# Gate and value products by Strassen's scheme in single PSUM banks, with twelve attention visits a batch

## Chip, cores, metric

One core of one Trainium2 chip. The metric is device microseconds of one execution. A ratio is the mean time of one kernel's fast runs over that of the other's fast runs of the same rounds, so it is not quite the ratio of the medians quoted.

## The reference

Sigmoid attention (8 batches, 12 heads, 448 tokens, head size 64), followed by a gated feed-forward over the 3584 tokens:

```python
scores = scale * q @ k.T - log(S);  attn = 1 / (1 + exp(-scores));  x = attn @ v
gate = maximum(x @ w_gate, 0);  val = x @ w_val        # x: 3584 x 768, w: 768 x 1536
out  = (gate * val) @ w_out                            # w_out: 1536 x 768
```

## The kernel before

The feed-forward of batch b and the attention of batch b + 1 are interleaved on TensorE: the loop over the feed-forward's matmuls calls `visit()` now and then. A "pass" is four 64x64 matmuls of scores and one sigmoid of 128x896. Three blocks of four heads make a batch; a block has seven score passes and seven value passes.

```python
def up(b, f, ...):                      # one chunk of 128 of d_ff: 6 gate + 6 value matmuls of 448
    for dc in range(NDC): gate = gv_part(b, f, wg, [dc]) ...
    nc.vector.tensor_scalar(out=g_sb, in0=gate, scalar1=0.0, op0=AOP.max)
    for dc in range(NDC): val = gv_part(b, f, wv, [dc]) ...
    nc.vector.tensor_tensor(out=hT[f][:, o:o+S], in0=g_sb, in1=val, op=AOP.mult)

def feed(i):                            # behind score pass i: what the next blocks need
    n, c = divmod(i, NCH); m = n + 1
    if c == 0 and NPRO <= m < NB: cast_block(m)                  # GpSimd
    ...
    if c == 3 and NPRO <= m < NB: dma_transposes(m)              # k, q of the next block, SP's queue
    if c == 3 and NPRO <= m + 1 < NB: load_all(m + 1)            # k, q, v of the one after, SP's queue

def visit():                            # three score passes, with the seven value passes when due
    ...
# per batch 7 visits (8 in batch 0), spread evenly over up() and down()
```

`down(col0)` makes 128 output rows (12 matmuls of 512, 12 of 256), VectorE evicts them and SP's queue stores them. Batches have alternately three and four such blocks: 0, 2, 4, 6 have three.

## Time and profile before

| | before |
|---|---|
| time | 429.98 us (429.91 to 430.1) |
| TensorE busy, share of the chain that ended last | 98%, 93% |
| VectorE, ScalarE, GpSimd busy | 39%, 42%, 24% |
| transposing transfers of k and q, issue to landing (median) | 3.0 us |

The chain that ended last is followed back from the last instruction, at each step to what released it. An issue is the instruction by which a queue starts a transfer; the transfer has landed when its data is there. In the lines below SPq is SP's queue, x18 a count, and L146 line 146 of the kernel.

```profile
105.30 1.23 SPq L146 DMA_TRANSPOSE kT<-h16k  x1
106.57 1.30 SPq L146 DMA_TRANSPOSE qT<-h16q  x1
107.92 0.58 SPq L90 DMA_DIRECT2D st_k<-in_k_dram  x1
108.54 0.48 SPq L90 DMA_DIRECT2D st_q<-in_q_dram  x1
109.07 0.47 SPq L90 DMA_DIRECT2D st_v<-in_v_dram  x1
```

```profile
kT<-h16k SPq DMA_TRANSPOSE x18, 3.0
qT<-h16q SPq DMA_TRANSPOSE x18, 3.0
```

The two transposes of the next block are issued first, then the three loads of the block after next, 1.4 MB.

### The profile page before, as it was taken

The page shows a single profiled execution, that of the slowest core. Times are in us where ns is not written, and L with a number is a line of the kernel's source. Part 1 is how long each engine was busy: PE and PEld are TensorE (multiplying, and loading weights), DVE is VectorE, ACT ScalarE, POOL GpSimd, SP SyncE. Part 2 cuts the span into 40 slices and gives each one's busy share as a digit, 9 for nine tenths or more (in the row PEclk, how much of TensorE's full clock was granted, in tenths as well). Part 3 has the DMA queues.
Part 4 walks back from the last instruction along what each step waited for, and adds up shares of the span by engine and source line. Part 5 has one row for each costly group of instructions (what it writes and reads, how often), then busy time and mean ns, then how long its engine had stood idle before and what let it go on. Part 6 is the DMA issues. An engine that isn't in the chain of part 4 may idle for free.

```text
span 428.4 us, 7873 instructions
## 1 busy us (share of the span) xinstructions
PE 418.1 (98%) x3282; PEld 216.5 (51%) x3282; DVE 166.5 (39%) x276; ACT 178.5 (42%) x217; POOL 102.2 (24%) x137
## 2 busy tenths in 40 slices
PE   7789999999999999999999999999999999999996
PEld 4334555544555445545455444554455544555553
DVE  3555542353323452244423444244422435235531
ACT  5952566525434445444343545443435363500000
POOL 2567683333300333013120233003330030000000
PEclk9999999999999999999999999999999999999999
DMA  8999996673535753386623666247443730030014
GB/s 303 384 385 385 390 373 155 184 196 115 160 98 103 205 149 113 78 206 174 170 50 94 179 173 173 73 95 207 121 150 98 181 72 0 20 93 0 2 37 110
DMA packets 64371, 66.96 MB, mean 156 GB/s; under 512 B 35792, under 2 KB 54608, under 8 KB 64336
## 3 DMA queue, kind: packets, MB, share of 16 engines
q1 hardware_dynamic: 63088, 64.63, 51.8%
q10 hardware_dynamic: 1248, 1.84, 1.2%
q8 instruction: 25, 0.41, 0.4%
q14 instruction: 10, 0.08, 0.1%
HBM read 47.19 MB, written 11.01 MB: 136 GB/s over the span
## 4 chain that ended last, share of the span: by engine, by line
PE 93%; ACT 3%; DMA 2%; DVE 1%; issue 0%; ACTq 0%; DVEq 0%
PE gv_ps L232 51%; PE y_ps L275 26%; PE qk_ps L173 8%; PE pv_ps L197 7%; ACT PT L183 3%; DMA st_q<-in_q_dram 2%; PE tr L159 1%; DVE ysb L289 0%; DVE gate_sb L249 0%; DVE xT L213 0%; DVE h16q L107 0%; ACT L367 0%; ACT xT L211 0%; ACTq L295 0%; ACTq L90 0%
## 5 line engine op out<-in xcount | busy, mean ns | idle before, releaser
L183 ACT ACTIVATE PT<-qk_ps,bias_t 128x896 f16<-128x896 f32 x168 | 159.2, 1008 | 191.1 <-PE qk_ps L173 191.1
L232 PE MATMUL gv_ps<-xT,wg 128*128 128x448 f16 x576 | 128.1, 353 | 0.4 <-ACT xT L211 0.2
L232 PE MATMUL gv_ps<-xT,wv 128*128 128x448 f16 x576 | 126.9, 353 | 0.0
L275 PE MATMUL y_ps<-wo,hT 128*128 128x512 f16 (+2 forms) x684 | 113.7, 323 | 0.0
L275 PEld LDWEIGHTS <-hT 128*128 128x128 f16 x684 | 64.6, 98 | 48.0 <-issue 6.3
L249 DVE TENSOR_SCALAR gate_sb<-gv_ps 128x448 f32<-128x448 f32 x96 | 59.9, 624 | 73.4 <-PE gv_ps L232 73.4
L256 DVE TENSOR_TENSOR hT<-gate_sb,gv_ps 128x448 f16<-128x448 f32 x96 | 59.6, 621 | 64.3 <-PE gv_ps L232 64.2
L232 PEld LDWEIGHTS <-wg 128*128 128x128 f16 x576 | 55.0, 98 | 55.7 <-issue 7.7
L232 PEld LDWEIGHTS <-wv 128*128 128x128 f16 x576 | 55.0, 98 | 54.8 <-issue 5.2
L289 DVE TENSOR_SCALAR ysb<-y_ps 128x512 f32<-128x512 f32 (+2 forms) x56 | 31.1, 555 | 105.3 <-PE y_ps L275 104.1
L107 POOL CAST h16q<-st_q 128x896 f16<-128x896 f32 x20 | 18.6, 930 | 220.0 <-DMA st_q<-in_q_dram 195.3
L173 PE MATMUL qk_ps<-qT,kT 64*64 64x448 f16 x672 | 48.6, 358 | 3.9 <-ACT PT L183 2.9
L197 PE MATMUL pv_ps<-PT,v 64*64 64x448 f16 x672 | 39.1, 350 | 0.8 <-ACT PT L183 0.7
L173 PEld LDWEIGHTS <-kT 64*64 64x64 f16 x672 | 16.5, 105 | 29.8 <-issue 22.7
L197 PEld LDWEIGHTS <-v 64*64 64x64 f16 x672 | 19.9, 107 | 12.7 <-issue 2.1
L211 ACT ACTIVATE xT<-pv_ps 128x448 f16<-128x448 f32 x43 | 21.0, 547 | 6.0 <-PE pv_ps L197 4.8
L287 ACT ACTIVATE ysb<-y_ps 128x128 f32<-128x128 f32 x1 | 0.3, 277 | 44.8 <-PE y_ps L275 44.8
L107 POOL CAST h16k<-st_k 128x896 f16<-128x896 f32 x20 | 18.6, 928 | 0.0
L114 POOL CAST v<-st_v 128x448 f16<-128x448 f32 x24 | 13.3, 556 | 10.3 <-DMA st_v<-in_v_dram 10.3
L115 POOL CAST v<-st_v 64x448 f16<-64x448 f32 x24 | 13.4, 558 | 1.5
L116 POOL CAST v<-st_v 64x448 f16<-64x448 f32 x24 | 13.3, 555 | 1.0
L139 POOL CAST wv<-st_wu 128x1536 f16<-128x1536 f32 x6 | 8.8, 1467 | 5.7 <-DMA st_wu<-in_moe_w_val_dram 5.7
(26 smaller groups left out, 59.3 us busy)
## 6 DMA issues: line engine op xcount, KB each, us to landing
out_dram<-ysb SPq DMA_DIRECT2D x54, 192.0 KB, 2.7
st_q<-in_q_dram SPq DMA_DIRECT2D x23, 448.0 KB, 4.5
st_v<-in_v_dram SPq DMA_DIRECT2D x23, 448.0 KB, 5.2
st_k<-in_k_dram SPq DMA_DIRECT2D x22, 448.0 KB, 4.0
st_wg<-in_moe_w_gate_dram SPq DMA_DIRECT2D x6, 768.0 KB, 12.3
st_wu<-in_moe_w_val_dram SPq DMA_DIRECT2D x6, 768.0 KB, 12.2
st_wo<-in_moe_w_out_dram SPq DMA_DIRECT2D x6, 768.0 KB, 12.1
st_v<-in_v_dram ACTq DMA_DIRECT2D x1, 448.0 KB, 5.8
```

What stands on the lines that cost most here:

```text
L107: eng.tensor_copy(o, i)
L114: eng.tensor_copy(t[:, 0], st[:, 0])
L115: eng.tensor_copy(t[0:64, 1], st[64:128, 1])
L173: nc.tensor.matmul(ps[o : o + 64, bank, 0:S], kT[r : r + 64, c, h, :], qT[r : r + 64, :, h, :], start=True, stop=True, tile_position=(r, o ...
L183: nc.scalar.activation(pt[:], ps[:, :, 0:S], AF.Sigmoid, bias=bias_t[:], scale=qk_scale)
L197: nc.tensor.matmul(pv[o : o + 64, pr, 0:S], t[r : r + 64, pr, c * D : (c + 1) * D], pt[r : r + 64, pr, :], start=(c == 0), stop=(c == NCH ...
L211: nc.scalar.activation(x[:], pv[:, pr, 0:S], AF.Copy, scale=XSCALE)
L232: nc.tensor.matmul(begun[key][:, 0:S], w[j][:, dc, jj * P : (jj + 1) * P], xT[b, dc][:], start=(dc == 0), stop=(dc == NDC - 1),)
L249: nc.vector.tensor_scalar(out=g_sb[:], in0=gate[:, 0:S], scalar1=0.0, scalar2=None, op0=AOP.max)
L256: nc.vector.tensor_tensor(out=hT[f][:, o : o + S], in0=g_sb[:], in1=val[:, 0:S], op=AOP.mult)
L275: nc.tensor.matmul(y[:, 0:w], hT[f][:, o : o + P], wo[f // FG][:, f % FG, c0 : c0 + w], start=(f == 0), stop=(f == NFC - 1),)
L289: nc.vector.tensor_scalar(out=dst, in0=y[:, 0:w], scalar1=OUT_SCALE, scalar2=None, op0=AOP.mult)
```

## The change

Intent: for batches 1 to 7, split the tokens (224 + 224), the contraction (384 + 384) and the outputs (gate, value) in halves and form the four results from seven half-size products instead of eight. The sums of weights are made once, in batch 0's output products; the sums of tokens once a batch; the seven products are combined by VectorE (five adds and one max-and-multiply per pair of chunks), ScalarE (a copy and a relu) and GpSimd (one multiply). The products need four single PSUM banks, so scores have two pairs of banks instead of three, so a visit has two score passes instead of three, and a batch twelve visits instead of seven.

```diff
-    qkp = ...(name="qkp", bufs=3, PSUM)   # pairs of banks: scores, values
-    wkp = ...(name="wkp", bufs=2, PSUM)   # single banks: gate, value, output
+    pairs = [psp.tile([P, 2, 512], FP32, name=f"pair{i}") for i in range(2)]
+    banks = [psp.tile([P, 512], FP32, name=f"bank{i}") for i in range(4)]
+        factors = {1: (A11, B(wg, 0)), 2: (A12, B(wg, 1)), 3: (S4, B(wv, 1)), 4: (A22, TT(4)),
+                   5: (S1, TT(1)), 6: (S2, TT(2)), 7: (S3, TT(3))}
+        todo = [(0, 1), (0, 6), (0, 7), (0, 2), (0, 5), (1, 1), (0, 3)]        # (pair of chunks, product)
+        for g in range(1, NG2):
+            todo += [(g, 6), (g - 1, 4), (g, 7), (g, 5), (g, 2)]
+            todo += [(g + 1, 1)] if g + 1 < NG2 else []
+            todo += [(g, 3)]
+        todo += [(NG2 - 1, 4)]
...
     def feed(i: int):
-        if c == 0 and NPRO <= m < NB:
-            cast_block(m)
-        if c == 3 and NPRO <= m < NB:
-            dma_transposes(m)
+        if NPRO <= m < NB:
+            if c == 0: cast_qk(m, "q", nc.gpsimd)
+            if c == 2: cast_qk(m, "k", nc.gpsimd)
+            if c == 4:
+                dma_transposes(m)
+                cast_v(m, nc.gpsimd)
         if c == 3 and NPRO <= m + 1 < NB:
             load_all(m + 1)
...
+            for _, may in gv_fast(b):                 # may: behind product 6 of each pair, six a batch
+                if may and b + 1 < B: visit()
+            todo = [0.3 + k * (total - 3.3) / 5 for k in range(6)]    # six more in the output products
```

More of the change, by code (lines that the diff above doesn't have):

```diff
@@ L49 @@
     wpool = ctx.enter_context(tc.tile_pool(name="wpool", bufs=1))
-    stp = ctx.enter_context(tc.tile_pool(name="stp", bufs=10))
+    stp = ctx.enter_context(tc.tile_pool(name="stp", bufs=9))
     swp = ctx.enter_context(tc.tile_pool(name="swp", bufs=5))
@@ L54, with next_pair, take, give @@
     qkTp = ctx.enter_context(tc.tile_pool(name="qkTp", bufs=4))
-    PTp = ctx.enter_context(tc.tile_pool(name="PTp", bufs=11))
-    xTp = ctx.enter_context(tc.tile_pool(name="xTp", bufs=2 * NDC))
-    gsbp = ctx.enter_context(tc.tile_pool(name="gsbp", bufs=3))
-    ysbp = ctx.enter_context(tc.tile_pool(name="ysbp", bufs=3))
-    qkp = ctx.enter_context(tc.tile_pool(name="qkp", bufs=3, space=bass.MemoryType.PSUM))
-    wkp = ctx.enter_context(tc.tile_pool(name="wkp", bufs=2, space=bass.MemoryType.PSUM))
+    PTp = ctx.enter_context(tc.tile_pool(name="PTp", bufs=8))
+    xTp = ctx.enter_context(tc.tile_pool(name="xTp", bufs=4))
+    sxp = ctx.enter_context(tc.tile_pool(name="sxp", bufs=1))
+    tmpp = ctx.enter_context(tc.tile_pool(name="tmpp", bufs=2))
+    ysbp = ctx.enter_context(tc.tile_pool(name="ysbp", bufs=2))
+    psp = ctx.enter_context(tc.tile_pool(name="psp", bufs=1, space=bass.MemoryType.PSUM))
+    pairs = [psp.tile([P, 2, 512], FP32, name=f"pair{i}") for i in range(2)]
+    banks = [psp.tile([P, 512], FP32, name=f"bank{i}") for i in range(4)]
+    held: set = set()
+    turn = {"pair": 0, "bank": 0, "banks": (0, 1)}
+    def next_pair():
+        turn["pair"] ^= 1
+        return pairs[turn["pair"]]
+    def take():
+        ids = turn["banks"]
+        for k in range(len(ids)):
+            i = ids[(turn["bank"] + k) % len(ids)]
+            if i not in held:
+                turn["bank"] = (turn["bank"] + k + 1) % len(ids)
+                held.add(i)
+                return i
+        raise AssertionError("no bank")
+    def give(i):
+        held.remove(i)
     bias_t = const.tile([P, 1], FP32, name="bias_t")
@@ L73 @@
     wo = [wpool.tile([P, FG, DM], FP16, name=f"wo{j}") for j in range(NG)]
-    hT = [wpool.tile([P, NHALF * S], FP16, name=f"hT{f}") for f in range(NFC)]
+    hT = [wpool.tile([P, 2, NHALF * S], FP16, name=f"hT{f}") for f in range(NFC // 2)]
     staged: dict = {}
@@ L87, in load_block @@
         for nm, src, c0, c1, eng in which:
-            st = stp.tile([P, 2, S], FP32, tag="st", name=f"st_{nm}")
+            if nm == "k2":
+                st = staged["k", n]
+            else:
+                st = stp.tile([P, 2, S], FP32, tag="st", name=f"st_{nm}")
             rows = src[b, i * HB : (i + 1) * HB].rearrange("(r h) (p c) d -> (h p) r (c d)", h=2, c=NCH)
@@ L153, in transposes @@
         if n <= NBLK:
-            tr = wkp.tile([P, NCH, 2, KC], FP16, tag="wk", name="tr")
-        else:
-            tr = qkp.tile([P, 2, 512], FP32, tag="qk", name="tr")[:, 0, 0 : S].bitcast(FP16)
-            tr = tr.rearrange("p (c h k) -> p c h k", c=NCH, h=2)
+            bank = take()
+            tr = banks[bank][:, 0:S]
+        else:
+            bank = None
+            tr = next_pair()[:, 0, 0:S]
+        tr = tr.bitcast(FP16).rearrange("p (c h k) -> p c h k", c=NCH, h=2)
         for c in range(cut[0], cut[-1]):
@@ L165, in transposes @@
                 eng.tensor_copy(t2[:, c0:c1], tr[:, c0:c1])
+        if bank is not None:
+            give(bank)
         qkT[nm, n] = t2
@@ L169, in scores @@
         qT, kT = qkT["q", n], qkT["k", n]
-        ps = qkp.tile([P, 2, 512], FP32, tag="qk", name="qk_ps")
+        ps = next_pair()
         for r, h, o, bank in ((0, 0, 0, 0), (0, 1, 64, 0), (64, 0, 64, 1), (64, 1, 0, 1)):
@@ L190, in values @@
         if chunks[0] == 0 and n not in PT:
-            PT[n] = qkp.tile([P, 2, 512], FP32, tag="qk", name="pv_ps")
+            if n < NBLK:
+                PT[n] = [banks[2][:, :], banks[3][:, :]]
+            else:
+                pair = next_pair()
+                PT[n] = [pair[:, 0], pair[:, 1]]
         pv = PT[n]
@@ L197, in values @@
                 nc.tensor.matmul(
-                    pv[o : o + 64, pr, 0:S],
+                    pv[pr][o : o + 64, 0:S],
                     t[r : r + 64, pr, c * D : (c + 1) * D],
@@ L208, in values @@
             for pr in range(2):
-                x = xTp.tile([P, S], FP16, tag="xT", name="xT")
+                dc = 2 * i + pr
+                if (b, 0) not in xT:
+                    for kh in range(2):
+                        xT[b, kh] = xTp.tile([P, NDC // 2, S], FP16, tag="xT", name="xT")
+                x = xT[b, dc // 3][:, dc % 3]
                 if n >= NBLK or (pr and n == NBLK - 1):
-                    nc.scalar.activation(x[:], pv[:, pr, 0:S], AF.Copy, scale=XSCALE)
+                    nc.scalar.activation(x, pv[pr][:, 0:S], AF.Copy, scale=XSCALE)
                 else:
-                    nc.vector.tensor_scalar(
-                        out=x[:], in0=pv[:, pr, 0:S], scalar1=XSCALE, scalar2=None, op0=AOP.mult
-                    )
-                xT[b, 2 * i + pr] = x
+                    nc.vector.tensor_scalar(out=x, in0=pv[pr][:, 0:S], scalar1=XSCALE, scalar2=None, op0=AOP.mult)
             PT.pop(n)
@@ L228, in gv_part @@
         if key not in begun:
-            begun[key] = wkp.tile([P, 512], FP32, tag="wk", name="gv_ps")
+            begun[key] = take()
         j, jj = divmod(f, FG)
@@ L232, in gv_part @@
             nc.tensor.matmul(
-                begun[key][:, 0:S],
+                banks[begun[key]][:, 0:S],
                 w[j][:, dc, jj * P : (jj + 1) * P],
-                xT[b, dc][:],
+                xT[b, dc // 3][:, dc % 3],
                 start=(dc == 0),
@@ L247, in up @@
                 yield MM_US
-        g_sb = gsbp.tile([P, S], FP32, tag="gsb", name="gate_sb")
-        nc.vector.tensor_scalar(out=g_sb[:], in0=gate[:, 0:S], scalar1=0.0, scalar2=None, op0=AOP.max)
+        g_sb = tmpp.tile([P, S], FP32, tag="r1", name="gate_sb")
+        nc.vector.tensor_scalar(out=g_sb[:], in0=banks[gate][:, 0:S], scalar1=0.0, scalar2=None, op0=AOP.max)
+        give(gate)
         yield MM_US
@@ L255, in up, with weight_sum @@
         o = (b % NHALF) * S
-        nc.vector.tensor_tensor(out=hT[f][:, o : o + S], in0=g_sb[:], in1=val[:, 0:S], op=AOP.mult)
+        nc.vector.tensor_tensor(
+            out=hT[f // 2][:, f % 2, o : o + S], in0=g_sb[:], in1=banks[val][:, 0:S], op=AOP.mult
+        )
+        give(val)
         yield MM_US
+    HS = S // 2
+    HDC = NDC // 2
+    T: dict = {}
+    Sx: dict = {}
+    def weight_sum(k: int, j: int):
+        B11, B21 = wg[j][:, 0:HDC], wg[j][:, HDC:NDC]
+        B12, B22 = wv[j][:, 0:HDC], wv[j][:, HDC:NDC]
+        if k == 3:
+            out, a, b = B12, B22, B12
+        else:
+            i = 3 * j + (1, 2, 4).index(k)
+            if i % 2 == 0:
+                T["tile"] = swp.tile([P, 2, HDC, FG * P], FP16, tag="sw", name="Tw")
+            out = T["tile"][:, i % 2]
+            a, b = {1: (B12, B11), 2: (B22, T.get((1, j))), 4: (B21, T.get((2, j)))}[k]
+        nc.vector.tensor_tensor(out=out, in0=a, in1=b, op=AOP.subtract)
+        T[k, j] = out
@@ new lines, in x_sum @@
+    def x_sum(b: int, k: int):
+        A11, A21 = xT[b, 0][:, :, 0:HS], xT[b, 0][:, :, HS:S]
+        A12, A22 = xT[b, 1][:, :, 0:HS], xT[b, 1][:, :, HS:S]
+        if k == 1:
+            Sx[b] = sxp.tile([P, 4, HDC, HS], FP16, tag="sx", name="Sx")
+        t = Sx[b]
+        a, c, op = {
+            1: (A21, A22, AOP.add),
+            2: (t[:, 0], A11, AOP.subtract),
+            3: (A11, A21, AOP.subtract),
+            4: (A12, t[:, 1], AOP.subtract),
+        }[k]
+        nc.vector.tensor_tensor(out=t[:, k - 1], in0=a, in1=c, op=op)
@@ new lines, in gv_fast, with B, TT, two @@
+    def gv_fast(b: int):
+        half = lambda t, h: [t[:, dc, h * HS : (h + 1) * HS] for dc in range(HDC)]
+        A11, A21 = half(xT[b, 0], 0), half(xT[b, 0], 1)
+        A12, A22 = half(xT[b, 1], 0), half(xT[b, 1], 1)
+        S1, S2, S3, S4 = ([Sx[b][:, k, dc] for dc in range(HDC)] for k in range(4))
+        def B(w, kh):
+            return lambda j, dc: w[j][:, kh * HDC + dc]
+        def TT(k):
+            return lambda j, dc: T[k, j][:, dc]
+        factors = {
+            1: (A11, B(wg, 0)),
+            2: (A12, B(wg, 1)),
+            3: (S4, B(wv, 1)),
+            4: (A22, TT(4)),
+            5: (S1, TT(1)),
+            6: (S2, TT(2)),
+            7: (S3, TT(3)),
+        }
+        o = (b % NHALF) * S
+        live: dict = {}
+        def two(t):
+            return t[:, 0:S].rearrange("p (f s) -> p f s", f=2)
+        def tmp(g, nm):
+            live[g, nm] = tmpp.tile([P, S], FP32, tag=nm, name=nm)
+            return live[g, nm]
+        def product(g, k):
+            a, w = factors[k]
+            nm = {1: "b1", 2: "b1", 6: "b2", 5: "b2", 3: "b2", 7: "b3", 4: "b3"}[k]
+            first = k in (1, 6, 7)
+            if first:
+                live[g, nm] = take()
+            i = live[g, nm]
+            bank = banks[i]
+            for fi in range(2):
+                j, jj = divmod(2 * g + fi, FG)
+                for dc in range(HDC):
+                    nc.tensor.matmul(
+                        bank[:, fi * HS : (fi + 1) * HS],
+                        w(j, dc)[:, jj * P : (jj + 1) * P],
+                        a[dc],
+                        start=(first and fi == 0 and dc == 0),
+                        stop=(dc == HDC - 1),
+                        skip_group_check=True,
+                    )
+                if fi == 0:
+                    yield 3 * MM_US / 2, False
+            ps = bank[:, 0:S]
+            add = lambda out, c: nc.vector.tensor_tensor(out=out[:], in0=ps, in1=c[:], op=AOP.add)
+            if k == 1:
+                nc.scalar.copy(tmp(g, "s1")[:], ps)
+            elif k == 6:
+                add(tmp(g, "s2"), live[g, "s1"])
+            elif k == 5:
+                add(tmp(g, "s4"), live[g, "s1"])
+                t = live[g, "s4"]
+                nc.vector.tensor_tensor(out=t[:], in0=banks[live[g, "b3"]][:, 0:S], in1=t[:], op=AOP.add)
+            elif k == 2:
+                nc.scalar.activation(tmp(g, "r1")[:], ps, AF.Relu)
+                give(i)
+            elif k == 3:
+                t = live[g, "s1"]
+                add(t, t)
+                give(i)
+                nc.gpsimd.tensor_tensor(
+                    out=hT[g][:, :, o : o + HS], in0=two(live[g, "r1"]), in1=two(t), op=AOP.mult
+                )
+            elif k == 4:
+                t = live[g, "s2"]
+                add(t, t)
+                give(i)
+                nc.vector.scalar_tensor_tensor(
+                    out=hT[g][:, :, o + HS : o + S],
+                    in0=two(t),
+                    scalar=0.0,
+                    in1=two(live[g, "s4"]),
+                    op0=AOP.max,
+                    op1=AOP.mult,
+                )
+            yield 3 * MM_US / 2, k == 6
+        NG2 = NFC // 2
+        todo = [(0, 1), (0, 6), (0, 7), (0, 2), (0, 5), (1, 1), (0, 3)]
[4 more added lines that the diff above has]
+        todo += [(NG2 - 1, 4)]
+        for g, k in todo:
+            yield from product(g, k)
@@ L266, in down @@
             w = mn // nb
-            if nb == 2:
-                yt = qkp.tile([P, 2, 512], FP32, tag="qk", name="y_ps")
-                ys = [yt[:, 0], yt[:, 1]]
-            else:
-                ys = [wkp.tile([P, 512], FP32, tag="wk", name="y_ps")]
+            ids = [take() for _ in range(nb)]
+            ys = [banks[i] for i in ids]
             for f in range(NFC):
@@ L276, in down @@
                         y[:, 0:w],
-                        hT[f][:, o : o + P],
+                        hT[f // 2][:, f % 2, o : o + P],
                         wo[f // FG][:, f % FG, c0 : c0 + w],
@@ L289, in down @@
                     nc.vector.tensor_scalar(out=dst, in0=y[:, 0:w], scalar1=OUT_SCALE, scalar2=None, op0=AOP.mult)
+                give(ids[j])
             if last or m0 + mn == DM:
@@ L300, in blocks128, with down_us @@
         return range(first, (b + 1) * S - P + 1, P)
-    def ffn(b: int):
-        for f in range(NFC):
-            if b == 0 and f == 0:
-                yield from up(b, f, 4, 3)
-            else:
-                yield from up(b, f)
-        for col0 in blocks128(b):
-            yield from down(col0)
-    def ffn_us(b: int) -> float:
-        return NFC * 2 * NDC * MM_US + len(blocks128(b)) * NFC * (DM / 2400.0 + 0.004)
+    def down_us(b: int) -> float:
+        return len(blocks128(b)) * NFC * (DM / 2400.0 + 0.004)
     NPRO = 2 * NBLK
@@ L325, in feed @@
         m = n + 1
-        if c == 0 and NPRO <= m < NB:
-            cast_block(m)
+        if NPRO <= m < NB:
+            if c == 0:
+                cast_qk(m, "q", nc.gpsimd)
+            if c == 2:
+                cast_qk(m, "k", nc.gpsimd)
+            if c == 4:
+                dma_transposes(m)
+                cast_v(m, nc.gpsimd)
         if c == 4 and NBLK < m < NPRO:
             later.append(m)
-        if c == 3 and NPRO <= m < NB:
-            dma_transposes(m)
         if c == 3 and NPRO <= m + 1 < NB:
@@ L335 @@
     later: list = []
-    valued: set = set()
-    state = {"pass": NBLK * NCH}
-    def visit():
-        i0 = state["pass"]
-        i1 = min(i0 + 3, NPASS)
-        n = i0 // NCH - 1
-        ready = n >= NBLK and n not in valued
-        for i in range(i0, i1):
-            if ready and i == i0 + 2:
-                values(n, range(NCH))
-            scores(*divmod(i, NCH))
-        if ready and i0 == NPASS:
-            values(n, range(NCH))
-        if ready:
-            valued.add(n)
-        for i in range(i0, i1):
+    visits = []
+    for n in range(NBLK, NB):
+        visits.append(([n - 1] if n > NBLK else [], [n * NCH]))
+        visits += [([], [n * NCH + c, n * NCH + c + 1]) for c in (1, 3, 5)]
+    visits.append(([NB - 1], []))
+    def visit():
+        pv, qk = visits.pop(0)
+        for n in pv:
+            values(n, range(NCH))
+        for i in qk:
+            scores(*divmod(i, NCH))
+        for i in qk:
             feed(i)
-        state["pass"] = i1
     zeros = const.tile([P, 512], FP16, name="zeros")
@@ L359, in filler @@
     def filler(*widths):
-        if 0 not in PT:
-            PT[0] = qkp.tile([P, 2, 512], FP32, tag="qk", name="pv_ps")
         for w in widths:
-            nc.tensor.matmul(PT[0][:, 0, 0:w], zeros[:, 0:P], zeros[:, 0:w], start=True, stop=True)
+            nc.tensor.matmul(banks[2][:, 0:w], zeros[:, 0:P], zeros[:, 0:w], start=True, stop=True)
     with tc.manual_schedule():
@@ L437 @@
                 start_next()
-        for b in range(B):
-            total = ffn_us(b)
-            todo = []
-            if b + 1 < B:
-                count = NBLK * NCH // 3 + (1 if b == 0 else 0)
-                lo = 6.0 if b == 0 else 0.0
-                todo = [lo + (k + 0.5) * (total - lo) / count for k in range(count)]
+        turn["banks"] = (0, 1, 2, 3)
+        gv_us = NFC * 2 * NDC * MM_US
+        total = gv_us + down_us(0)
+        lo = 6.0
+        todo = [lo + k * (total - lo - 3.0) / 12 for k in range(13)]
@@ new lines, with ffn0 @@
+        sums = []
+        wsums = [(k, j) for j in range(NG) for k in (1, 2, 4, 3)]
+        t = 0.0
+        due = 0.0
+        def ffn0():
+            for f in range(NFC):
+                if f == 0:
+                    yield from up(0, f, 4, 3)
+                else:
+                    yield from up(0, f)
+            for col0 in blocks128(0):
+                yield from down(col0)
+        for step, cost in enumerate(ffn0()):
+            t += cost
+            if order and step % 8 == 0:
+                start_next()
+            if todo and t >= todo[0]:
+                due = todo.pop(0) + 2.0
+                visit()
+                if not todo:
+                    sums = [1, 2, 3, 4]
+            if later and t >= due:
+                m = later.pop(0)
+                transposes(m, "k")
+                transposes(m, "q")
+            if wsums and t >= gv_us and step % 5 == 0:
+                assert not order
+                weight_sum(*wsums.pop(0))
+            if sums and not todo and t >= total - 1.5:
+                x_sum(1, sums.pop(0))
@@ L446 @@
+        for a in wsums:
+            weight_sum(*a)
+        for part in sums:
+            x_sum(1, part)
+        for b in range(1, B):
+            for _, may in gv_fast(b):
+                if may and b + 1 < B:
+                    visit()
+            total = down_us(b)
+            todo = [0.3 + k * (total - 3.3) / 5 for k in range(6)] if b + 1 < B else []
+            sums = [1, 2, 3, 4] if todo else []
             t = 0.0
-            for step, cost in enumerate(ffn(b)):
+            for cost in (c for col0 in blocks128(b) for c in down(col0)):
@@ L448 @@
                 t += cost
-                if order and step % 8 == 0:
-                    start_next()
                 if todo and t >= todo[0]:
-                    due = todo.pop(0) + 2.0
+                    todo.pop(0)
                     visit()
-                if later and t >= due:
-                    m = later.pop(0)
-                    transposes(m, "k")
-                    transposes(m, "q")
-            for _ in todo:
-                visit()
+                if sums and t >= total - 1.5:
+                    x_sum(b + 1, sums.pop(0))
@@ L462 @@
+            for part in sums:
+                x_sum(b + 1, part)
+        assert not visits and not held
 _INS = ['q', 'k', 'v', 'moe_w_gate', 'moe_w_val', 'moe_w_out']
```

## The prediction

> **What bounds the kernel now.** I read the page first: busy shares, then the chain that ended last, then the groups. TensorE is busy 98% and is 93% of the chain; the granted clock is 0.998.
>
> ```profile
> PE 418.1 (98%) x3282; PEld 216.5 (51%) x3282; DVE 166.5 (39%) x276; ACT 178.5 (42%) x217; POOL 102.2 (24%) x137
> PE 93%; ACT 3%; DMA 2%; DVE 1%; issue 0%; ACTq 0%; DVEq 0%
> L183 ACT ACTIVATE PT<-qk_ps,bias_t 128x896 f16<-128x896 f32 x168 | 159.2, 1008 | 191.1 <-PE qk_ps L173 191.1
> L256 DVE TENSOR_TENSOR hT<-gate_sb,gv_ps 128x448 f16<-128x448 f32 x96 | 59.6, 621 | 64.3 <-PE gv_ps L232 64.2
> ```
>
> So only work taken off TensorE counts. The gate and value products are 51% of the chain (218 us), so I need their true spacing; the mean of 353 ns per matmul is start to end, of pipelined work. The chain in order of time gives it without overlap. The last batch has no attention beside it:
>
> ```profile
> 381.56 27.24 PE gv_ps L232 x144
> 408.80 14.30 PE y_ps L275 x84
> ...
> 83.34 6.16 PE gv_ps L232 x32
> 89.50 0.69 PE qk_ps L173 x12
> 90.19 6.16 PE gv_ps L232 x32
> 96.35 0.50 PE qk_ps L173 x8
> 96.85 1.32 PE pv_ps L197 x28
> 98.18 0.19 PE qk_ps L173 x4
> ```
>
> 27.24/144 = 189.2 ns for 448 columns: 448/2.4 = 186.7 ns plus 2.5 ns. Attention is 0.189 us for each four 64x64 matmuls (1.32/7; 0.19), and a visit of three score passes takes 0.69 where 3 x 0.189 = 0.57 would do. In the engines' busy time by stretches, two whole batches (the pattern repeats at 79.43, 180.33 and 281.2) last 100.9 us with TensorE never idle. Their parts: 288 gate/value matmuls x 0.1892 = 54.5; 7 output blocks x 12 x (0.2158 + 0.1091) = 27.3; 42 score and 42 value passes x 0.189 = 15.9; sum 97.7. The 3.2 us left, over 14 visits, is 0.23 us a visit.
>
> Does a narrower matmul keep that fixed 2.5 ns, when each needs its own weights and a weight load is listed at 98 ns? The timeline of the start has seven transposes, 128 columns each with fresh weights, and the timeline of the end a run with 128-wide halves:
>
> ```profile
> 12.05 0.56 PE L159 MATMUL tr<-ident,h16q 128*128 128x128 f16 x7
> ...
> 423.10:424.40 1.30, 1.30 (x24) 0.69 (x1) 0.00 (x0) 1.00 0.47 144
> ```
>
> (0.56 less a 0.17 us pipeline tail)/7 = 56 ns, and 1.30/24 = 54 ns. Weight loads do not limit at 56 ns, so 224 columns should run at 93.3 + 2.5 = 95.9 ns.
>
> **What the Trainium skill says.** "TensorE: Matmul & The Clock Gate", Back-to-back issue gap: N/2.4 + 2.5 ns for an isolated warm matmul, but 81 ns at N = 128 in a stream of load-and-matmul pairs. The trace agrees with the first (189.2, 56) and not with the 81. "TensorEngine Tiling (Array Packing)", Key Properties: changing the tiling mode drains TensorE; the 0.23 us a visit agrees. "VectorE: DVE Perf Modes", the perf-mode tier table: tensor_tensor goes at double rate only for 16-bit data in SBUF, single for fp32 or PSUM. The trace shows the second (448 elements in 621 ns), none of the first. "SBUF — State Buffer", Who interferes with whom: a VectorE instruction with two SBUF inputs and a GpSimd instruction that reads SBUF block each other for a whole instruction. No VectorE instruction here has two SBUF inputs, so this trace can't say.
>
> **Part 1, the products (removed from the path).** Before, a pair of f chunks takes 24 matmuls of 448. After, 7 products x 2 chunks x 3 contraction chunks = 42 matmuls of 224. A batch: 144 x 0.1892 = 27.24 against 252 x 0.0959 = 24.17, so 3.07 us saved. The ideal eighth would be 3.41; the rest goes to the 2.5 ns being paid 252 times. Seven batches: **-21.5 us**.
>
> **Part 2, the visits (added to the path).** Before there are 8 + 6 x 7 = 50 visits, after 13 + 6 x 12 = 85. The passes are the same; 35 more mode changes x 0.23 = **+8.1 us**. The pure TensorE sum is -13.4 us: **416.6 us**, my floor.
>
> **Part 3, the combining (moved to VectorE, ScalarE, GpSimd).** Per chunk pair VectorE had 4 instructions of 0.62; now it has five PSUM adds and one SBUF max-and-multiply, 6 x 0.62 = 3.7 us, and ScalarE a copy and a relu (0.55 each, as its xT copies), GpSimd one two-input multiply (estimate: twice its 556 ns one-input cast, 1.1 us). TensorE takes 42 x 0.0959 = 4.03 us a pair, 4.6 with a two-score visit, so VectorE fits with 80 to 92% load. It must also fit in order. From the end of product 4: result visible +0.20 (in the timeline a gate eviction starts 0.20 after the last matmul would free TensorE), add 0.62, then max-and-multiply to 1.49, then the add on product 5, done at 2.11 plus some 0.06 for the signal. Product 3, which adds into the same bank, is due after four products, at 2.30. So nominally nothing is lost, but the slack is only 0.13 us. GpSimd casts fall in five of a batch's six chunk pairs (0.93 for q or k, three of 0.56 for v), and the max-and-multiply has two SBUF inputs: where it lands on a cast it waits 0.3 to 0.5 us, of which 0.2 to 0.4 reaches TensorE. Taking one or two such hits a batch at 0.2 us: about 0.25 a batch, **+1.5 us**, could be 5.
>
> **Part 4, the weight sums (once).** Twelve 16-bit subtractions of 1536 elements in the output products of batch 0. Estimate from the skill's double rate: 768/0.96 + 70 to 150 ns = 0.87 to 0.96 each, 11 us. In the same stretch, about 65 to 80 us by the new order, VectorE has 6 evictions (3 us) and two token sums (0.4 each) before the second product of batch 1 can start, and GpSimd casts there for 3.5 us (65.1 to 68.6 before), which I count as lost to VectorE. Sum 18.3 us against TensorE's 3 blocks x 3.9 + three visits of 0.61 + one of 1.74 = 15.3, plus 0.58 for the first product. So TensorE waits about 2.5 us: **+2.5**. At single rate (1.67 each) it would be +11.
>
> **Part 5, the boundaries.** Later token sums depend on the last visit, 3.0 us before the end of the output products. The two xT copies on ScalarE finish 0.2 + 1.1 us after its value passes, 1.9 us before the end counting its score pass, and the first two sums take 0.9: hidden. In the even batches (three output blocks) visits come every 1.68 + 0.6 = 2.3 us and ask 2 x 1.03 us of sigmoids through two PSUM pairs in place of three: 0.05 to 0.1 us lost now and then. In the prologue the value bank is no longer rotated, but its eviction (two of 0.62) ends about when the old wait for a rotating buffer ended (value pass at 18.03): nothing. I put +0.4 on all this. Transfers fall no closer: transposes and loads are issued by a queue that runs ahead, and DMA is at half load after 64 us.
>
> Sum: 429.98 - 21.5 + 8.1 + 1.5 + 2.5 + 0.4 = **421.0 us**, 2.1% less.
>
> **Rivals.** (A) *VectorE becomes the bound.* For: 80 to 92% load, a three-instruction chain with 0.13 us slack, possible blocking by GpSimd. Against: the trace shows back-to-back VectorE instructions starting 0.535 us apart, closer than their 0.62 duration, so the load is nearer 80%. If each of 42 chunk pairs lost 0.3 us: +12, about 432. (B) *Narrow matmuls are limited by weight loads.* For: the listed load of 98 ns is longer than 95.9. Against: the 54 and 56 ns runs. If 98 ns were a floor, 1764 x 2.1 ns = +3.7 on the sum, 424.7; at 107 ns all 19.6 us would be gone, about 440. (C) *Only the mode changes cost*, everything else hides: 416.6. (D) *The weight sums run at single rate*: 421 + 8.5 = 429.5. I hold (C) and a mild (A) as the likeliest neighbours.
>
> **Range and chances.** The floor of 416.6 needs no stall at all; 416.0 leaves half a microsecond for mis-sized terms. Above, a mild (A) and a heavier boundary together add 5 to 8: **416.0 to 428.0**. The 2% line is 421.4, just over my centre, and the errors lean to the slow side, but a change with so finely placed visits and sums was evidently tuned against such waits. Chances: faster by over 2% 0.50, within 2% 0.46, slower by over 2% 0.04 (it would need B at 107 ns or a full A, 438.6 or more).
>
> **What would show it.** Right: the last batch's 252 products in some 24.2 us of the chain; PT passes in 85 visits with 0.23 us of extra each; VectorE around 60% busy in all and near 75 to 85% in the product stretches; a gap of 2 to 3 us once, between batches 0 and 1, released by VectorE; waits of TensorE's product line on VectorE of 1 to 3 us in all otherwise. Wrong: product spacing at 98 ns or over (B); TensorE waiting 0.2 us or more in nearly every chunk pair (A); weight subtractions of 1.7 us (D); waits of scores on sigmoids in every even batch, which would mean that two PSUM pairs are too few.

## The result, and the profile after

441.17 us median (440.43 to 442.12), against 429.95: ratio 1.0262, interval 1.0239 to 1.0284. **Slower by 2.6%**, outside the predicted range of 416 to 428. The page after, busy shares and the chain:

```profile
PE 413.0 (94%) x4038; PEld 283.2 (65%) x4038; DVE 241.6 (55%) x400; ACT 227.2 (52%) x301; POOL 156.9 (36%) x179
...
PE 70%; DVE 5%; DMA 5%; SPq 3%; issue 1%; ACTq 0%; ACT 0%; DVEq 0%
```

The chain's shares sum to 84% only: it could be followed back no further than 70.8 us, so 70% is not to be compared with the 93% before. New on it are transposed q (DMA, 5%) and SP's queue (3%); the 2% of DMA before was a load at the start. VectorE is at 55%: it is not the bound. Who waited for whom (total, times, longest), TensorE's rows:

```profile
PE pair L205 <- DMA qT<-h16q: 12.6, 3, 4.5
PE pair L205 <- ACT PT L215: 2.9, 8, 0.7
PE bank L378 <- DVE s L389: 1.3, 7, 0.2
...
PE bank L378 <- DVE Sx L334: 0.9, 1, 0.9
```

Three waits, of 3.8 to 4.5 us, for a transposed q: one each in the output products of batches 0, 2 and 4, the batches with three blocks that still have blocks to fetch. SP's queue and TensorE around the second (an entry in brackets is the idle time before it and its releaser):

```profile
174.07 1.12 SPq L466 DMA_DIRECT2D out_dram<-ysb  x2
175.24 0.59 SPq L118 DMA_DIRECT2D st_k<-in_k_dram  x1
175.88 0.51 SPq L118 DMA_DIRECT2D st_q<-in_q_dram  x1
176.43 0.51 SPq L118 DMA_DIRECT2D st_v<-in_v_dram  x1
177.04 1.72 SPq L174 DMA_TRANSPOSE kT<-h16k  x1
178.81 2.90 SPq L174 DMA_TRANSPOSE qT<-h16q  x1
```

```profile
179.67 1.52 PE L233 MATMUL pair<-PT,v 64*64 64x448 f16 x28
185.56 0.38 PE L205 MATMUL pair<-qT,kT 64*64 64x448 f16 x4 [4.38 <-DMA qT<-h16q]
185.88 4.67 PE L445 MATMUL bank<-wo,hT 128*128 128x512 f16 x19
```

The order has turned: the three loads now stand in front of the transposes. The transposes land 6.3 us after issue instead of 3.0:

```profile
kT<-h16k SPq DMA_TRANSPOSE x18, 6.3
qT<-h16q SPq DMA_TRANSPOSE x18, 6.3
```

The issue itself has lengthened too, for qT from a median of 1.30 us to 2.90. The queue did not run ahead either: it stood behind the store of an output block (174.07) that VectorE finished at 174.04. And the wait costs more than its length. The engines' busy time by stretches has the granted clock (1.00 is full) in its third column from the right:

```profile
182.00:184.00 2.00, 0.00 (x0) 0.00 (x0) 0.00 (x0) 0.22 (x1) 1.15 (x2) 1.00 1.45 99
...
186.00:188.00 2.00, 2.00 (x7) 0.68 (x6) 0.00 (x0) 1.01 (x1) 0.00 (x0) 0.59 0.00 0
188.00:190.00 2.00, 2.00 (x11) 1.33 (x10) 1.32 (x3) 0.00 (x0) 0.00 (x0) 0.56 0.00 0
```

After the idle stretch TensorE gets 0.59 and 0.56 of its clock. These are means over 2 us: a finer stretch, 186.5 to 189.5, reads 0.50. The same follows the wait in batch 4 (0.50 from 291 to 295), but not the one of 3.75 us in batch 0. The Trainium skill, "TensorE: Matmul & The Clock Gate", Part 1, says that a clock gate halves the clock after an idle window of some 3.4 us; the trace agrees with the halving, less with the length (see the last section).

Batch by batch, from the start of the first product of one to that of the next in TensorE's timeline: batches 2 and 4 take 53.68 and 54.5 us; batch 6, which also has three blocks but no transposes left to wait for, takes 47.24. So these two waits cost 6.4 and 7.3 us.

### The profile page after: what moved, and what is told of

Read it like the earlier page. It is cut to its first block, busy times and chain, and to the rows that moved or that the text cites. A ratio compares the mean times of both kernels' runs of the same rounds, so it can differ in the third digit from the quotient of the medians.

```text
span 438.9 us, 9698 instructions
## 1 busy us (share of the span) xinstructions
PE 413.0 (94%) x4038; PEld 283.2 (65%) x4038; DVE 241.6 (55%) x400; ACT 227.2 (52%) x301; POOL 156.9 (36%) x179
## 4 chain that ended last, share of the span: by engine, by line
PE 70%; DVE 5%; DMA 5%; SPq 3%; issue 1%; ACTq 0%; ACT 0%; DVEq 0%
PE bank L378 36%; PE bank L445 21%; PE pair L205 7%; PE pair L233 5%; DMA qT<-h16q 5%; DVE s L389 3%; SPq L174 1%; SPq L118 1%; DVE hT L412 1%; SPq L466 1%; DVE ysb L459 1%; DVE wv L319 0%; DVE Sx L334 0%; ACTq L466 0%; ACT ysb L457 0%
## 5 line engine op out<-in xcount | busy, mean ns | idle before, releaser
L215 ACT ACTIVATE PT<-pair,bias_t 128x896 f16<-128x896 f32 x168 | 160.5, 1006 | 85.7 <-PE pair L205 85.6
L389 DVE TENSOR_TENSOR s<-bank,s 128x448 f32<-128x448 f32 x168 | 102.3, 622 | 47.2 <-PE bank L378 46.4
L445 PE MATMUL bank<-wo,hT 128*128 128x512 f16 (+2 forms) x684 | 121.5, 331 | 0.0
L405 POOL TENSOR_TENSOR hT<-r,s 128x448 f16<-128x448 f32 x42 | 47.7, 1135 | 183.8 <-DVE s L389 173.3
L378 PEld LDWEIGHTS <-Tw 128*128 128x128 f16 x756 | 70.3, 98 | 12.5 <-issue 11.8
L205 PE MATMUL pair<-qT,kT 64*64 64x448 f16 x672 | 52.5, 363 | 16.8 <-DMA qT<-h16q 12.6
L378 PE MATMUL bank<-Sx,wv 128*128 128x224 f16 x504 | 62.0, 259 | 2.3 <-DVE s L389 1.3
L378 PE MATMUL bank<-Sx,Tw 128*128 128x224 f16 x504 | 62.0, 259 | 0.9 <-DVE Sx L334 0.9
L378 PE MATMUL bank<-xT,wg 128*128 128x224 f16 x504 | 57.4, 259 | 0.0
L233 PE MATMUL pair<-PT,v 64*64 64x448 f16 x588 | 31.9, 352 | 0.0
```

Of the source, the lines that this page charges most:

```text
L205: nc.tensor.matmul(ps[o : o + 64, bank, 0:S], kT[r : r + 64, c, h, :], qT[r : r + 64, :, h, :], start=True, stop=True, tile_position=(r, o ...
L215: nc.scalar.activation(pt[:], ps[:, :, 0:S], AF.Sigmoid, bias=bias_t[:], scale=qk_scale)
L233: nc.tensor.matmul(pv[pr][o : o + 64, 0:S], t[r : r + 64, pr, c * D : (c + 1) * D], pt[r : r + 64, pr, :], start=(c == 0), stop=(c == NCH ...
L378: nc.tensor.matmul(bank[:, fi * HS : (fi + 1) * HS], w(j, dc)[:, jj * P : (jj + 1) * P], a[dc], start=(first and fi == 0 and dc == 0), sto ...
L389: add = lambda out, c: nc.vector.tensor_tensor(out=out[:], in0=ps, in1=c[:], op=AOP.add)
L405: nc.gpsimd.tensor_tensor(out=hT[g][:, :, o : o + HS], in0=two(live[g, "r1"]), in1=two(t), op=AOP.mult)
```

## The experiments

Theory 1: loads in front of the transposes. Rivals: the closer visits alone leave too little time; the issue time in the queue rather than the transfers; and for what remains, VectorE.

### 1. Transposes ahead of the loads

```diff
             if c == 4:
                 dma_transposes(m)
                 cast_v(m, nc.gpsimd)
-        if c == 3 and NPRO <= m + 1 < NB:
+        if c == 4 and NPRO <= m + 1 < NB:
             load_all(m + 1)
```

> The changed kernel with one edit: the three loads of the block after next are issued after the two transposing transfers of the next block, not before them. Theory 1 (the transposes queue behind 1.4 MB of loads: 1.7 us of issue and 3 to 4 us of transfer): they land in about 3.0 us again (6.3 median in the changed kernel), TensorE never waits for them, the three stalls of batches 0, 2 and 4 go (about 5, 6.5 and 7.4 us with the slow clock after them), and the time is about 422 us (419 to 424). Theory 2 (order does not matter; 12 visits in a three-block stretch leave too little time because the issuing queue is held behind the output stores): landing stays near 6 us, about 1.7 us of each stall goes with the earlier issue, time 432 to 437.

A visit takes passes 3 and 4 together and feeds both at its end, so the edit only swaps the order of issue within one visit. Measured: 425.77 us (424.56 to 428.62), ratio 0.9913. TensorE's waits for a transfer are gone, and landing is back:

```profile
kT<-h16k SPq DMA_TRANSPOSE x18, 3.4
qT<-h16q SPq DMA_TRANSPOSE x18, 3.0
```

In the same stretch the transposes still stand behind the store (174.41), but qT, issued at 177.00, lands at 180.01, 1.3 us before its score pass. So theory 1 holds and theory 2 does not, though the time is above the 419 to 424 expected. Part of that is the clock: runs at a granted clock of 0.992 took 428.6, at 1.000 425.0 and less. In the profiled run (0.992) the clock halves twice: in the prologue (0.50 from 24 to 27 us, with no wait there over 0.71 us), and after TensorE has waited 2.06 us for a token sum of batch 1 (0.50 from 85.5 to 88.5).

### 2. Loads through another queue

```diff
-            load_all(m + 1)
+            for nm, src in (("k", k), ("q", q), ("v", v)):
+                load_block(m + 1, (nm, src, 0, NCH, nc.scalar))
```

> The changed kernel with the loads in their place in the program, but issued by ScalarE's queue. If what delays the transposes is the loads' 1.7 us of issue ahead of them on the one queue, the time is near 422 to 425. If it is the shared transfer engines working off 1.4 MB of loads, the transposes still land in 5 to 6 us, the stalls shrink by 1 to 2 us each and the clock stays up, 430 to 436. ScalarE pays some 0.5 us of its sequencer per load, 55 loads, off the path of TensorE.

Measured: 445.33 us (441.58 to 445.9), slower than the change itself and above both expectations. SP's queue now issues the transposes right behind the store, at 176.51 and 177.87 us in the stretch of batch 2 shown above for the change, but ScalarE's queue issues the loads at 176.82 to 178.65, and the two share the transfer engines. Landing of qT (minimum, median, maximum):

```profile
DMA to landing us min/median/max: 2.9/3.0/10.9
```

The three transposes of q that TensorE waits for take 8.0 to 10.9 us, the other fifteen 2.9 to 4.9. So the loads need not stand in front of them in the one queue: loads in transfer beside them delay them as well, and more. This agrees with the Trainium skill, "DMA: Bandwidth & Descriptors", Issuing engines are not separate DMA queues: all issuers' transfers run on the same 16 engines and interleave.

### 3. Something to do in the wait

19 matmuls of zeros into a free bank, in front of the score pass that waits:

```diff
         for n in pv:
             values(n, range(NCH))
+        if fill:                     # 19 in the last visit of batches 0, 2 and 4
+            i = take()
+            for _ in range(fill):
+                nc.tensor.matmul(banks[i][:, 0:512], zeros[:, 0:P], zeros[:, 0:512], start=True, stop=True)
+            give(i)
```

> The changed kernel with 19 matmuls of zeros, 4.1 us of work, in front of the score pass that stalls in batches 0, 2 and 4. They do nothing for the result and fall in time that TensorE spends idle. If part of the loss is the lower clock after an idle stretch of over 4 us (granted clock 0.57 to 0.59 for some 4 to 5 us after the stalls of batches 2 and 4), the clock stays near 0.998 and the time falls by about 4 us to 437. If the clock is no part of it, the time stays at 441 or rises.

Measured: 437.82 us (437.33 to 439.72), clock 0.999. As expected: useless work makes the kernel 3.4 us faster. So of the 17 us that the stalls cost (see 5), some 3.4 are the lower clock. The stretch after the wait in batch 2, now at full clock:

```profile
186.50:190.50 4.00, 4.00 (x33) 2.83 (x33) 1.99 (x5) 1.10 (x2) 0.00 (x0) 1.00 0.07 28
```

### 4. The same order in the kernel before

```diff
-        if c == 3 and NPRO <= m < NB:
-            dma_transposes(m)
         if c == 3 and NPRO <= m + 1 < NB:
             load_all(m + 1)
+        if c == 3 and NPRO <= m < NB:
+            dma_transposes(m)
```

> The kernel before with only the order of the change: loads of the block after next ahead of the transposes of the next. If order alone makes the stall, the transposes land in 6 us instead of 3.0 and the time rises by 5 us or more. If it needs the close visits of the change too (2.3 us apart in three-block batches, against 6 us apart before), landing goes to 5 to 6 us, but the time stays within 0.5%, 430 to 432.

Measured: 441.62 us (438.83 to 442.95), ratio 1.027. The first branch holds: the wider spacing of the visits does not hide it. Swapping two statements in the old kernel costs 11.8 us, as much as the whole change. TensorE waits six times for qT (7.9 us in all, up to 2.4, and after that one the clock reads 0.50 for 3.4 us), landing goes to 5.5 (k) and 5.0 us (q). So the closer visits are not needed for the stall; the order suffices.

### 5. Moving the transposes instead of the loads

```diff
             if c == 2:
                 cast_qk(m, "k", nc.gpsimd)
+                dma_transposes(m)
             if c == 4:
-                dma_transposes(m)
                 cast_v(m, nc.gpsimd)
```

> The changed kernel with its loads where they are, and the transposes issued one visit earlier, right behind the cast of k, so ahead of the loads in the queue. If the order of loads and transposes is the whole cause, it gives what e1 gives, 425 us, whichever of the two is moved; landing 3.0 us, no wait of TensorE on them. As GpSimd's q cast then does not move onto the token sums (in e1 at 282 us), 424 rather than 425.

Measured: 424.11 us (424.0 to 424.44), ratio 0.986, the runs within 0.1%. Landing 3.3 and 3.0 us. It does not matter which of the two is moved. The change less this is 17.1 us: the price of the order (15.4 by experiment 1, part of whose runs had the lower clock).

### 6. One load in front

```diff
+        if c == 4 and NPRO <= m + 1 < NB:
+            load_all(m + 1, "kq")            # behind the transposes
         if c == 3 and NPRO <= m + 1 < NB:
-            load_all(m + 1)
+            load_all(m + 1, "v")             # still in front
```

> The changed kernel with one load (v, 0.46 MB) left ahead of the transposes and two put behind them. If what delays the transposes is the bytes in front of them, they land in 3.8 to 4.5 us (3.0 with none in front, 6.3 with three), TensorE waits at most 1 us in the three-block batches and the clock stays up: 425 to 428 us. If a single transfer in front already makes the transposes wait (a switch between the two kinds of transfer), landing is near 6 us and the time 435 or more.

Measured: 430.26 us (429.39 to 431.37), ratio 0.9991. Landing medians are 5.1 and 4.7 us, between the 3.3 and 3.0 of none in front and the 6.3 of three, and TensorE's waits are 5.4 us, the longest 2.6, between 0 and 12.6. The first half of the expectation holds in direction, though it was under-sized: a third of the bytes makes about half of the delay, the longest wait is over 1 us, the time is above 425 to 428, and in the profiled run the clock halved once. A switch between kinds of transfer as the whole cause (landing near 6 us, 435 or more) is out; a fixed part beside one that grows with the loads is not.

### 7. Plain products with twelve visits

The kernel of experiment 1 with `up()` in all batches and no sums of weights or tokens:

```diff
-            for _, may in gv_fast(b):
+            for _, may in gv_plain(b):       # up(b, f) for all f; a visit in every second chunk
```

> The kernel of e1 with plain products (144 matmuls of 448) in batches 1 to 7 and no sums of weights or tokens, but the 12 visits a batch and the single banks of the change. My terms: the visits add 8.1 us, Strassen takes 21.5 away. So this kernel should be at 430.0 + 8.1 = 438 us (437 to 439), and e1 less this one is the worth of the products with all that they bring, -21.5 plus the stalls. If a visit costs nothing like 0.23 us, it is at 430 to 433.

Measured: 439.13 us (438.72 to 441.56). The visits cost 9.2 us against the kernel before; predicted were 8.1. The chain shows it directly:

```profile
135.34 0.50 PE pair L205 x8
135.85 4.65 PE bank L269 x24
```

0.50 for two passes of 0.189, and 4.65 for 24 x 0.1893 = 4.54: 0.12 + 0.11 = 0.23 us a visit. Against this kernel, experiment 1 (same visits, same order of transfers, Strassen) is 13.4 us faster.

### 8. Four weight sums later; 9. that and 5 together

```diff
-        wsums = [(k, j) for j in range(NG) for k in (1, 2, 4, 3)]
+        wsums = [(k, j) for j in range(NG - 1) for k in (1, 2, 4, 3)]
+        late = [(k, NG - 1) for k in (1, 2, 4, 3)]
 ...
+                if may and late:
+                    weight_sum(*late.pop(0))
```

> The kernel of e1_transposes_first, with the last four of the twelve weight sums moved from batch 0's output products into the first four chunk pairs of batch 1, one behind each visit. In e1 the first token sum of batch 1 came late behind the weight sums: TensorE waited 2.2 us, then 5 us at a clock of 0.66. If the wait is VectorE's backlog, it goes, and the low clock with it: 422 to 423 us. If it is something else (the xT copy, a GpSimd cast on the shared port), the wait stays and the time stays at 425, or rises, as VectorE is nearly full in the product stretches.

> f2 and the deferred weight sums of f1 together: 421 to 422.5 us if the two losses add up, with no wait of TensorE over 0.5 us from batch 0's products on and a clock of 0.998 or more.

Measured: 426.3 us (425.0 to 427.68) and 425.23 us (424.85 to 427.57), no better than without. The wait on the token sum at batch 1's start shrinks (in f3 from 1.7 to 0.5 us), but VectorE seems to have no room for sums in the pairs after the first: TensorE's waits on the adds rise from 1.3 to 2.6 us, and the product stretch of batch 1, from its first product to the first output matmul in TensorE's timeline, takes 32.0 us in place of 31.5. A miss.

### 10. The edges of a batch

In the chain of experiment 5, a batch's product stretch:

```profile
233.87 1.84 PE bank L378 x18
235.72 0.02 issue
235.74 0.64 DVE s L389
236.37 0.04 issue
236.42 1.31 PE bank L378 x12
237.73 0.50 PE pair L205 x8
238.23 4.13 PE bank L378 x42
242.36 0.50 PE pair L205 x8
...
258.64 0.02 issue
258.67 0.64 DVE s L389
259.30 0.02 issue
259.33 0.62 DVE hT L412
259.95 0.55 DVE s L389
260.50 0.04 issue
260.54 1.40 PE bank L378 x12
```

In the middle 42 products take 4.13 us, which is 42 x 0.0959 and 0.10 for the mode change: nothing is lost. In the first and last pair the chain runs over VectorE. There only one product stands between 5 and 3, and product 3 adds into the bank that the add on 5 still reads. New order:

```diff
-        todo = [(0, 1), (0, 6), (0, 7), (0, 2), (0, 5), (1, 1), (0, 3)]
+        todo = [(0, 1), (0, 6), (0, 7), (0, 5), (0, 2), (1, 1), (0, 3)]
 ...     # last pair
-            todo += [(g, 6), (g - 1, 4), (g, 7), (g, 5), (g, 2)]
+            todo += [(g, 6), (g, 7), (g, 5), (g, 2), (g - 1, 4)]
```

> f2_transposes_one_visit_earlier with another order of products in the first and the last chunk pair of each batch, so that two products stand between product 5 and product 3 as in the others (before, one). In f2 each batch loses 0.30 and 0.35 us there, TensorE waiting for the VectorE add on product 5. If that is the cause of the 0.75 us a batch over my sum, seven batches give about 4.3 us: 419.8 us, against 424.1. If something else holds TensorE at the edges (the token sums, the mode change), the wait moves to another product and the time stays at 423 to 424.

Measured: 420.54 us (420.24 to 420.73), ratio 0.9771. TensorE's waits on these adds fall from 1.3 us in 7 to 0.6 in 2, and the same two places in the chain:

```profile
232.31 3.56 PE bank L378 x36
235.86 0.50 PE pair L205 x8
...
256.09 3.56 PE bank L378 x36
259.65 0.43 PE bank L447 x2
```

36 products at 0.0959 are 3.45, and the mode change 0.10. The edges are worth 3.6 us.

### 11. One weight sum later; 12. with the edges

Experiment 5 with only the last weight sum behind the first visit of batch 1, and then with the order of experiment 10 too.

```diff
+        wsums = [...][:-1];  late = [(3, NG - 1)]
```

> f2 with only the twelfth weight sum moved behind the first visit of batch 1, where VectorE was idle for 1.6 us in f2. The wait of TensorE on the second token sum was 1.9 us in f2; one weight sum is 0.87 to 0.95 us. If the wait is the length of VectorE's queue, it shrinks to about 1 us: 423.2 us. Four sums moved (f1, f3) gave nothing, as they fell into full stretches.

> g1 and g2 together: 419 us (418.5 to 420), 2.5% under the kernel before, if the two add up.

Measured: 423.25 us (422.98 to 424.61) and **419.32 us (418.87 to 420.77), ratio 0.9753**, interval 0.973 to 0.9777. Both as expected, though the first is 0.9 us, close to its spread. The last kernel beats both the kernel before and the change: 2.5% under the one, 5% (21.85 / 441.17) under the other.

## Why the prediction was wrong

**The step that failed** is in Part 5: "Transfers fall no closer: transposes and loads are issued by a queue that runs ahead, and DMA is at half load after 64 us." Both halves are wrong. The queue runs ahead only as far as the next store, which waits for VectorE's eviction; that alone costs nothing (experiment 1 has it too, with 1.3 us to spare), but it leaves no time for three loads in front. And a mean DMA load says nothing about what stands in front of a small transfer that someone waits for: these landed in 6.3 us instead of 3.0, and TensorE waited 12.6 us. The diff moved `dma_transposes` from pass 3 to pass 4 and left `load_all` at pass 3; I read it as the same transfers a pass later. The price is 17.1 us (experiments 1 and 5 undo it, 4 makes it in the old kernel). It turns a kernel that is 1.4% faster into one that is 2.6% slower. My expected 421.0 plus 17.1 is 438.1; the other 3 us are mostly in parts 2 and 3. The chance of 0.04 for this outcome was meant for rival B or a full rival A; neither came.

**Part 1, right.** The last batch's products run at 16.85/174 = 96.8 ns in the chain of the change, 95.9 predicted, and 42 in the middle of a batch fit 95.9 once the mode change is taken off (experiment 10); rival B (weight loads as a floor) is out. One reading under it was off: the 54 ns of the run at the end is 56 by its timeline.

**Part 2, right in mechanism, a little small:** 9.2 us measured with plain products against 8.1. That kernel has other differences from the one before too (single banks, order of casts), so the last microsecond isn't assigned.

**Part 3, mis-sized.** I counted steady pairs, with 1.5 us for blocking on the shared port. Steady pairs lose nothing. The blocking itself occurs: of the 42 max-and-multiplies in the change, 29 take 0.62 us, and the 13 longer ones, up to 1.17, all start while a GpSimd instruction runs and end 0.48 us after it. But the chain shows no gap there. What I left out were the first and last pair of every batch: 0.30 + 0.35 us each, 4.5 us in seven batches, of which experiment 10 gets 3.6 back.

**Part 4, right in the rate, a little large in the wait.** A weight sum of 1536 elements takes 0.95 us, so at double rate; the wait was predicted as 2.5 us and is 0.9 us in the change (where the stall just before gave VectorE time to catch up), 1.7 us in experiment 5, 2.1 us in experiment 1.

**Rival A** (VectorE as the bound) did not come: 55% busy. Its small kin at the edges did.

So without the stalls: 416.6 + 4.5 (edges) + 1.7 (token sum) = 422.8, with about 1.1 us more for the visits, is near the 424.1 of experiment 5.

What stays open: how exactly plain loads and transposes share the transfer engines (loads in front delay, and loads beside delay more; no run here separates engines, or bytes from the number of transfers), and why the clock falls in some runs of the same kernel and not in others.

## What to carry to other kernels

When a diff moves a small transfer that an engine will wait for, list what is ahead of it in its queue and on the shared transfer engines, and compare with before, even where the mean DMA load is low. A stall of 2 us or more on TensorE can cost more than its length, because the clock mostly halved after it here. In a software pipeline of products, work out the first and last turn as well as the steady one: there the distances between dependent steps are shorter.

## What the Trainium skill lacked or had wrong

- "TensorE: Matmul & The Clock Gate", Back-to-back issue gap, gives 81 ns a matmul for 128 columns in a stream of weight loads and matmuls. Here seven 128-wide transposes with fresh weights took 56 ns each, and 174 products of 224 columns 96.8 ns each: the isolated formula (55.8 and 95.8 ns) holds in these streams to 1%.
- "TensorEngine Tiling (Array Packing)", Key Properties, says that a mode change drains TensorE, but not what it costs: 0.12 us on entering and 0.11 on leaving the 64x64 mode beside 128x128 work.
- "TensorE: Matmul & The Clock Gate", Part 1, puts the fall of the clock at an idle window of 3.4 us that runs freely, so one wait of 3.75 us followed by full clock does not speak against it. Too short for it are the waits of 2.06, 2.39 and 2.18 us (experiments 1, 4, 6) after which the clock read 0.50, and the fall in experiment 1's prologue without any wait over 0.71 us. Of the ten waits of 2 us or more in the profiled runs (2.06 to 6.49), eight went with a fall to 0.50, for 3.4 or 6.8 us; waits of 1.0 to 1.75 us did not.
- "DMA: Bandwidth & Descriptors" has no figure for a transposing transfer beside plain loads: 3.0 us alone, 4.7 to 5.1 behind one load of 448 KB, 6.3 behind three, up to 10.9 with three issued beside it from another queue.
